# Key projection of a 32-head attention kernel: eight heads in one product instead of four heads in column strips

## The chip, the cores and the metric

The kernel runs on one core of a Trainium2 chip. The metric is the device time of one execution in microseconds (us); times of several executions are given as their median. A profile is the record of one execution. Engines are named as the profile names them: PE (TensorE, matrix products), PEld (its weight loads), DVE (VectorE), ACT (ScalarE), POOL (GpSimd) and SP (SyncE, which here only issues DMAs).

## What is computed

One input x of 2048 rows and 512 columns (bf16) goes through two attention blocks with 32 heads of 16 columns each, and a gate per row mixes the two results.

```python
q, k, v = (x @ wqkv) split into 32 heads of 16            # for A and for B, each with its own wqkv
A: scores = q k^T / 4; p = softmax(scores); o = p v       # full, 2048 x 2048 for each head
B: the same over 8 keys per row: row s sees s, s-2, ..., s-14
a = o_A @ A_wo;  b = o_B @ B_wo
g = sigmoid(sum(x * gate_w))
out = g * a + (1 - g) * b
```

Block A holds nearly all the work: 32 heads of 2048 by 2048 scores, each of which needs one exponential.

## The kernel before, in words

**Units and sets.** The 32 heads are eight groups of four (group i holds heads 4i to 4i+3), and the 2048 query rows are four chunks of 512 (QW). A period is one group with one chunk; there are 32 periods, all eight groups of chunk 0 first. A period has 64 units: one unit is 128 keys of one head against the 512 queries. For each unit PE computes scores into one PSUM bank, an engine takes the exponential, and PE multiplies the result with the values and sums into the accumulator bank of the period. ACT does 1709 of the 2048 units in 684 activations (L1314, here "exps", counted from 0 as ex0, ex1, ...), alternately of three and of two units; the two PSUM rings `rA` (three banks) and `rB` (two) hold their scores, so that one is filled while the other is read. DVE does the other 339 units by integer arithmetic (L1242, L1261). Period 1 begins at ex24, period 2 at ex48, period 3 at ex72, period 4 at ex95, period 5 at ex118, period 6 at ex140, period 7 at ex162.

**The other three PSUM banks** ("misc") are shared by everything else: the accumulator of the running period (two at a change of period), all projections, the scores of DVE's units, transposes. A bank is given back when DVE has copied it out.

**Keys.** A score product takes 32 of PE's 128 rows (a row strip, one for each of four heads). In those 32 rows of `kt_all` a head has its 16 key rows and 16 *bound rows*: rows that hold minus the largest absolute key entry, one for each column. They meet |q| in the query tile, so that the product comes out as the score less an upper bound of it, and the exponential can't overflow. `k_proj` (L644) projects the keys of one group and one chunk: four contraction steps, and in each, four products of 32 output columns, one in each column strip of the array (`mm_k`, L378). 16 of the 32 columns of a strip are the head's own keys, the other 16 are those of a neighbour head and serve the bound. `kc` (L656) copies the bank into `kt_all` and takes the row maxima along. `k_bound` (L663) reduces the maxima, moves them to the right rows by two tiny products with `perm`, and `fill` (L679) writes them over the 16 bound rows. Heads 3 of the groups need a weight tile of their own, `wk3`, which DVE and POOL copy at the start (`k3`, L587).

**Queries.** From period 2 on, `q_pair` (L788) projects the queries of two groups at once: eight heads of 16 columns fill all 128 output columns, with the plain slice of `wq` as weights. DVE copies out q (`qs`) and |q| (`qa`), SP writes both to a scratch tensor in DRAM (`put`, L811, one DMA each), and two more DMAs (`get`, L818) read each group's 128 rows back, q and |q| interleaved per head.

**What sets the order.** Every piece of work is an `op` with an engine, a guessed duration, a due time (`dl`), an earliest time (`rel`), what it depends on and which buffers it takes. `list_schedule` (L175) runs through guessed time and, per engine, takes from the operations that can start the one that is due first; the instructions are then emitted in that order, and each engine executes its own in order. Keys of group i are due 14 us (by the guess) ahead of their first period and may not start before 12 us ahead of the start of the previous group (L699). Where PE would stand idle by the guess, the planner puts in products with zeros (L1472) that keep PE active.

Of the kernel before, what the change touches and what calls it, by code (L numbers as in the profile page):

```python
# [9 lines left out]
ALU = mybir.AluOpType  # L10
AX = mybir.AxisListType
FP32 = mybir.dt.float32
BF16 = mybir.dt.bfloat16
# [14 lines left out]
DH = 16  # L28
NG = 8
W = 8  # L30
DIL = 2
QW = 512
# [4 lines left out]
DEXP = -2.0565  # L37
NV = 4
NGR = 3
ROW = QW + 2  # L40
NPT = 3
NGA = 3
# [9 lines left out]
def _ap(base, dims):  # L52
    return bass.AP(tensor=base.tensor, offset=base.offset, ap=[list(d) for d in dims])
# [53 lines left out]
SB = lambda n: [(True, 0.065 + n / 3840.0)]  # L107
# [4 lines left out]
WAVE = lambda n: PASS * n  # L112
# [189 lines left out]
def kernel(  # L302
# [15 lines left out]
    S, D = x2d.shape  # L318
    assert D == 512 and S % QW == 0
    NT = S // 128  # L320
    NC = S // QW
    DC = D // 128
# [6 lines left out]
    const = ctx.enter_context(tc.tile_pool(name="const", bufs=1))  # L329
# [5 lines left out]
    def misc_ps(shape, dtype=FP32, tag="misc"):  # L335
        if tag in ("misc", "acc"):
            bank, = [tk.bank for tk in now[0].alloc if isinstance(tk.res, Banks)]
            tag = f"m{bank}"
        return ps.tile(shape, dtype, tag=tag, bufs=1, name="misc_ps")
# [27 lines left out]
    V = Chained(nc.vector, "dve")  # L367
    A = Chained(nc.scalar, "act")
    G = Chained(nc.gpsimd, "pool")
    SP = Chained(nc.sync, "sp")  # L370

    def mm(out, lhsT, rhs, start, stop, **kw):
        return chain(nc.tensor.matmul(out, lhsT=lhsT, rhs=rhs, start=start, stop=stop, **kw))  # L373
# [16 lines left out]
    def op(eng, occ, fn, dl, **kw):  # L390
        if any(tk.kind == "misc" for tk in kw.get("use", ())):
            dl -= URG[eng]
        o = Op(eng, occ, fn, dl, **kw)
        ops.append(o)
        return o
# [3 lines left out]
    def tok(tag, cap):  # L399
        name = "banks" if tag in ("misc", "acc") else tag  # L400
        if name not in res:
            res[name] = Banks(3) if name == "banks" else Res(cap)
        return Tok(res[name], tag)
# [53 lines left out]
    S0 = [T0 + UNIT * f for f in first_unit]  # L457

    wkv = const.tile([128, DC, 2 * D], BF16, name="wkv")
    wq = const.tile([128, DC, D], BF16, name="wq")  # L460
    wq2 = const.tile([128, DC, 8, 2, DH], BF16, name="wq2")
    q_scr = tc.dram_tile([NG * NC // 2 * 16, DH * QW], BF16, name="q_scr")
    wk3 = const.tile([128, DC, NG, 2, DH], BF16, name="wk3")
    a_w3 = A_wqkv.rearrange("(c p) n -> p c n", p=128)
    gw = const.tile([128, DC], BF16, name="gw")
    bw = const.tile([128, DC, 3 * D], BF16, name="bw")
    bwo = const.tile([128, DC, D], BF16, name="bwo")
# [7 lines left out]
    rowc = const.tile([128, 3], FP32, name="rowc")  # L475
    wts = const.tile([128, NV - 1], BF16, name="wts")
    z32 = const.tile([128, 32], BF16, name="z32")
    z_bc = _ap(z32[:, 0:1], [list(z32[:].ap[0]), [0, QW]])
    perm = const.tile([128, 2, 4, 2, DH], BF16, name="perm")
    qmask = const.tile([128, 1], U32, name="qmask")  # L480
    xT = const.tile([128, DC, S], BF16, name="xT")
    kt_all = const.tile([128, NG, S], BF16, name="kt_all")
    vp_all = const.tile([128, NT, H, DH + 1], BF16, name="vp_all")
    vd_all = const.tile([128, NV - 1, NTD, H, DH + 1], BF16, name="vd_all")
    kmax_all = const.tile([128, NG, NC], FP32, name="kmax_all")
    kmax_b = const.tile([128, NG], BF16, name="kmax_b")
    negk = const.tile([128, NG], FP32, name="negk")
# [29 lines left out]
    def init_perm():  # L517
        idv = ident[:].rearrange("p (a b d) -> p a b d", a=4, b=2)
        G.memset(perm[:], 0.0)
        G.tensor_copy(out=perm[:, 0, :, 1, :], in_=idv[:, :, 0, :])  # L520
        G.tensor_copy(out=perm[:, 1, 1:4, 1, :], in_=idv[:, 0:3, 1, :])
        G.tensor_copy(out=perm[:, 1, 0, 1, :], in_=idv[:, 3, 1, :])

    def init_pool2():
        make_identity(nc, identf)
# [11 lines left out]
    o_perm = op("pool", 1.0, init_perm, -8.5, deps=[o_id])  # L537
    o_init_p = op("pool", 2.8, init_pool2, -8.0, deps=[o_perm])
# [37 lines left out]
    o_wk = op("sp", 0.5, load_w(1), -8.9, lat=6.5)  # L576
# [10 lines left out]
    def k3(E, i0, i1):  # L587
        def s():
            wk = wkv[:, :, 0:D].rearrange("p c (i j d) -> p c i j d", i=NG, j=4)
            for e, j in ((0, 3), (1, 0)):  # L590
                E.tensor_copy(out=wk3[:, :, i0:i1, e, :], in_=wk[:, :, i0:i1, j, :])
        return s
# [6 lines left out]
        return s  # L599

    o_k3 = [op("dve", 0.2, k3(V, 0, 1), -4.0, deps=[o_wk])]
    o_k3 += [op("pool", 2.0, k3(G, 1, NG), -3.0, deps=[o_wk, o_init_p])] * (NG - 1)
    o_q2 = [op("dve", 0.5, q2(V, 0), 0.0, deps=[o_wq]), op("pool", 1.5, q2(G, 1), 5.0, deps=[o_wq, o_k3[1]])]

    def warm():
# [5 lines left out]
    o_xt = []  # L611
    for sc in range(NC):
        st = {}
# [76 lines left out]
            o_k[i] = [op("dve", 0.0, fill(0, S), dl, deps=[c], parts=SB(S))] * NC  # L690

    o_k = {}
    for i in range(NG):
        o_kc[i] = []
        for sc in range(NC):
            if i == 0:
                o_kc[i].append(k_proj(i, sc, ("misc", "acc", "misc", "misc")[sc], -2.0 + sc))
            else:
                o_kc[i].append(k_proj(i, sc, "misc", S0[i] - 14.0 - 3.5 * (NC - 1 - sc), rel=S0[i - 1] - 12.0 if i > 1 else K1REL))  # L699
        k_bound(i, 2.0 if i == 0 else S0[i] - 11.0)  # L700
# [87 lines left out]
    def q_pair(pi, dl, rel):  # L788

        c_, i = periods[pi]  # L790
        st = {}
        tk, tqs, tqa = tok("misc", 2), tok("qs", 1), tok("qa", 1)

        def part(c0, c1):
            def s():
                if c0 == 0:
                    st["p"] = misc_ps([128, QW])
                for c in range(c0, c1):
                    mm(st["p"][:], wq[:, c, 4 * i * DH:4 * (i + 2) * DH], xT[:, c, c_ * QW:(c_ + 1) * QW], c == 0, c == DC - 1)
            return s  # L800

        def ev():
            st["s"] = work.tile([128, QW], BF16, name="qs", tag="qs", bufs=1)
            V.tensor_copy(out=st["s"][:], in_=st["p"][:])

        def ab():
            st["a"] = work.tile([128, QW], BF16, name="qa", tag="qa", bufs=1)
            V.tensor_scalar(out=st["a"][:].bitcast(U32), in0=st["s"][:].bitcast(U32), scalar1=0x7FFF7FFF, scalar2=None,
                            op0=ALU.bitwise_and)

        def put(e):  # L811
            def s():
                src = st["sa"[e]]
                SP.dma_start(out=_ap(q_scr[8 * pi + e:8 * pi + e + 1, :], [[2 * DH * QW, 8], [QW, DH], [1, QW]]),
                             in_=src[:])
            return s

        def get(e):  # L818
            def s():
                qt_tiles[pi + e] = work.tile([128, QW], BF16, name="qt", tag="qt", bufs=4)  # L820
                SP.dma_start(out=qt_tiles[pi + e][:], in_=_ap(q_scr[8 * (pi + e):8 * (pi + e) + 1, :], [[QW, 128], [1, QW]]))
            return s
        a = op("pe", WAVE(2), part(0, 2), dl - 8.6, full=2, deps=[o_wq] + o_xt[c_], alloc=[tk], rel=rel, name=f"qp{pi}")
        a = op("pe", WAVE(2), part(2, DC), dl - 8.0, full=2, deps=[a], use=[tk], name=f"qp{pi}")
        c = op("dve", 0.61, ev, dl - 7.0, deps=[a], alloc=[tqs], use=[tk])
        b = op("dve", 0.0, ab, dl - 6.8, deps=[c], alloc=[tqa], use=[tqs], parts=SB(QW))
        w = [op("sp", 0.5, put(0), dl - 5.0, deps=[c], use=[tqs], lat=2.2), op("sp", 0.5, put(1), dl - 4.0, deps=[b], use=[tqa], lat=2.2)]
        for e in range(2):
            q_tok[pi + e] = tok("qt", 4)
            o_q[pi + e] = op("sp", 0.5, get(e), dl - 1.0 + e, deps=w, alloc=[q_tok[pi + e]], lat=2.2)  # L830
# [34 lines left out]
    a = None  # L865
    for sc in range(NC):
        a = op("pe", 0.9, zmm(sc), GT + sc, full=1, deps=[o_bw, a] + o_xt[sc], alloc=[tzp] if sc == 0 else [],
               use=[tzp] if sc else [], rel=20.0)
    a = op("act", 0.25, zsig, GT + 5, deps=[a], use=[tzp])
    o_g = op("dve", 0.8, zgate, GT + 6, deps=[a])  # L870
    a = op("pe", 1.2, zrows, GT + 8, full=1, deps=[o_g, o_init_p], alloc=[tzr])
# [427 lines left out]
    for k, us in enumerate(sets):  # L1299
# [6 lines left out]
        st = dict(k=k, us=us, tn=tn, tp=tp)  # L1306
# [7 lines left out]
        def ex(st=st, n=n, k=k):  # L1314
# [4 lines left out]
        a = op("pe", 0.0, qk, tn - 3.0, mode="r", js=[u_[2] for u_ in us], deps=[o_q[pi] for pi in pis] + kd,  # L1319
               alloc=[tr_], use=[q_tok[pi] for pi in pis], after=[last_qk[0]], scores=k % 2, name=f"qk{k}")  # L1320
# [15 lines left out]
    for pi, (c_, i) in enumerate(periods):  # L1336
        st = {}
# [32 lines left out]
        a = op("dve", 0.64, po1, E - PO1D, deps=o_pv[pi], alloc=[ta], use=[acc_tok[pi], acc_two[pi]])  # L1370
        tr_ = tok("rden", 2)
        a = op("dve", 0.29, po2, E + 4.0, deps=[a], alloc=[tr_], use=[ta])
        al, us = [to] if i % 2 == 0 else [], [ta, tr_] + ([to] if i % 2 else [])
        if by_v:
            a = op("dve", 0.0, po2a, E + 4.0, deps=[a, o_gr], use=[tr_], parts=TT(BPC))
            a = op("dve", 0.0, po2b, E + 4.0, deps=[a], alloc=al, use=us, parts=TT(BPC * DH))
        else:
            a = op("pool", 0.0, po2a, GFIRST, deps=[a, o_gr], use=[tr_], parts=GP("ff", BPC))
            a = op("pool", 0.0, po2b, GFIRST, deps=[a], alloc=al, use=us, parts=GP("ff", BPC * DH))
# [12 lines left out]
    for t in range(NT):  # L1392
        c_, tt = t // TPC, t % TPC
        st = {}
# [122 lines left out]
```

## Time and profile before

| what | value |
|---|---|
| median of 3 runs | 815.02 us (814.9 to 815.13) |
| profiled execution, its own time | 816.37 us |
| profiled execution, span from first to last instruction | 814.6 us |
| mean granted PE clock | 0.997 of full |
| ACT busy | 786.8 us (97%), of it 778.7 us in 684 exps |
| PE busy | 754.1 us (93%), 6969 products recorded |
| DVE busy | 685.0 us (84%) |
| POOL busy | 633.1 us (78%) |
| ex0 starts, last exp ends | 18.5 us, 806.6 us |

The profiled execution took 1.8 us more than its span, and 1.35 us more than the median of the runs. An engine's share of busy time is a mean over the whole span; in the first 215 us, in which all keys and values are projected, PE has more to do than later.

### The profile page before, as it was taken

The numbers are of one execution on the slowest core, as the hardware profiler recorded it, in microseconds if no ns is written. First come the engines' busy times: TensorE is split into PE (matmuls) and PEld (weight loads), VectorE is DVE, ScalarE is ACT, GpSimd is POOL, SyncE is SP. The second block draws the span as 40 slices with busy tenths as digits, with TensorE's granted clock in tenths as the row PEclk, the third lists the DMA queues.
The fourth block names the chain that finished last, engine by engine and source line by source line (L and its number), as shares of the span: only waits on it lengthen the run. The fifth ranks groups of instructions, "written<-read, shape, count | busy, mean of one in ns | idle before, by whom it ended". The sixth has DMA issues, their size and how long they took to land.

```text
span 814.6 us, 18016 instructions
## 1 busy us (share of the span) xinstructions
PE 754.1 (93%) x6969; PEld 247.2 (30%) x7022; DVE 685.0 (84%) x1068; ACT 786.8 (97%) x708; POOL 633.1 (78%) x1058
## 2 busy tenths in 40 slices
PE   8989999999999999989899999899989998999997
PEld 5343333323222222222232222223222222322322
DVE  5636787787988999989988899998989699999796
ACT  3999999999999999999999999999999999999996
POOL 3097979997998999999997894979789219998910
PEclk9999999999999999999999999999999999999999
DMA  8503081544344354444524516162442321522000
GB/s 261 140 5 118 2 180 42 149 111 104 93 100 127 104 118 130 110 112 107 132 54 111 136 33 163 34 162 54 91 130 50 81 86 58 144 59 72 1 2 27
DMA packets 58886, 77.22 MB, mean 95 GB/s; under 512 B 3744, under 2 KB 50848, under 8 KB 58800
## 3 DMA queue, kind: packets, MB, share of 16 engines
q1 hardware_dynamic: 52608, 53.91, 21.4%
q0 software_dynamic: 6048, 22.02, 14.8%
q8 instruction: 55, 0.90, 0.5%
q14 instruction: 31, 0.25, 0.1%
q10 hardware_dynamic: 144, 0.13, 0.0%
HBM read 43.78 MB, written 10.26 MB: 66 GB/s over the span
## 4 chain that ended last, share of the span: by engine, by line
ACT 49%; PE 24%; issue 21%; DVE 3%; DMA 2%; SPq 1%; ACTq 0%; DVEq 0%
ACT pT L364 48%; PE misc_ps L373 16%; PE ring L373 8%; DMA xld<-in_A_x_dram 1%; ACT lg L364 1%; SPq L364 1%; DMA woarr<-in_A_wo_dram 0%; DVE pd_a L364 0%; DMA q_scr<-qa 0%; DVE accT L364 0%; PE pxt L621 0%; DVE qs L364 0%; DVE qa L364 0%; DVE kt_all L364 0%; DVE kvs L364 0%
## 5 line engine op out<-in xcount | busy, mean ns | idle before, releaser
L364 ACT ACTIVATE pT<-ring 128x1536 bf16<-128x1536 f32 (+1 forms) x684 | 778.7, 1329 | 12.1 <-PE ring L373 9.3
L373 PE MATMUL ring<-qt,kt_all 32*128 32x512 bf16 x1709 | 268.7, 382 | 46.7 <-ACT pT L364 39.0
L364 POOL TENSOR_TENSOR prod<-ksh,qb 128x256 f32<-128x256 bf16 x256 | 174.0, 729 | 58.0 <-DMA ksh<-kv_scr 53.2
L373 PE MATMUL misc_ps<-pT,vp_all 128*17 128x512 bf16 (+1 forms) x1709 | 205.6, 384 | 1.7 <-DVE accT L364 1.1
L373 PEld LDWEIGHTS <-kt_all 32*128 32x128 bf16 x2048 | 88.2, 91 | 294.9 <-issue 286.4
L364 DVE TENSOR_SCALAR pd_a<-wkv 128x1536 uint16<-128x1536 uint16 x192 | 175.0, 941 | 0.9 <-PE misc_ps L373 0.4
L364 POOL TENSOR_TENSOR prod<-prod 128x256 f32<-128x256 f32 (+1 forms) x256 | 167.2, 668 | 5.6
L364 DVE TENSOR_SCALAR wkv<-misc_ps 128x512 uint16<-128x512 f32 x192 | 128.7, 683 | 26.8 <-PE misc_ps L373 24.1
L373 PE MATMUL misc_ps<-z 128*32 128x512 bf16 x425 | 138.2, 387 | 1.6 <-DVE z L364 1.6
L364 DVE TENSOR_SCALAR pd_a<-dt_a 128x1536 uint16<-128x1536 uint16 x147 | 135.2, 943 | 1.8 <-PE misc_ps L373 1.1
L373 PE MATMUL misc_ps<-pd_a,vd_all 128*17 128x512 bf16 x1017 | 130.9, 381 | 0.4 <-DVE pd_a L364 0.2
L373 PE MATMUL misc_ps<-qt,kt_all 32*128 32x512 bf16 x339 | 124.2, 381 | 1.3 <-DVE kt_all L364 0.4
L364 DVE TENSOR_SCALAR dt_a<-misc_ps 128x512 uint16<-128x512 f32 x147 | 98.8, 683 | 26.6 <-PE misc_ps L373 25.0
L364 POOL TENSOR_TENSOR prod<-vsh,lg 128x256 f32<-128x256 bf16 x128 | 84.2, 758 | 0.0
L373 PEld LDWEIGHTS <-vp_all 128*17 128x17 bf16 (+1 forms) x2048 | 55.1, 88 | 87.0 <-issue 73.2
L364 POOL TENSOR_TENSOR av<-vsh,lg 128x256 f32<-128x256 bf16 x128 | 78.2, 646 | 0.0
L373 PE MATMUL misc_ps<-bw,xT 128*128 128x512 bf16 x164 | 51.7, 389 | 1.1 <-issue 0.5
L373 PEld LDWEIGHTS <-z 128*32 128x32 bf16 x425 | 37.5, 96 | 48.2 <-issue 24.8
L373 PEld LDWEIGHTS <-vd_all 128*17 128x17 bf16 x1017 | 34.5, 88 | 48.2 <-issue 39.4
L373 PEld LDWEIGHTS <-xT 128*128 128x128 bf16 x576 | 29.1, 97 | 34.0 <-issue 31.0
L373 PE MATMUL misc_ps<-xT,wkv 128*32 128x512 bf16 x384 | 36.6, 381 | 0.0
L373 PE MATMUL misc_ps<-xT,wk 128*32 128x512 bf16 x128 | 35.8, 381 | 0.0
(89 smaller groups left out, 554.0 us busy)
## 6 DMA issues: line engine op xcount, KB each, us to landing
ksh<-kv_scr SPq DMA_DIRECT2D x32, 512.0 KB
vsh<-kv_scr SPq DMA_DIRECT2D x32, 512.0 KB
av<-prod POOLq DMA_DIRECT2D x28, 512.0 KB, 5.7
av<-av POOLq DMA_DIRECT2D x14, 512.0 KB, 5.3
kv_scr<-kvs SPq DMA_DIRECT2D x16, 256.0 KB
qt<-q_scr SPq DMA_DIRECT2D x30, 128.0 KB
q_scr<-qs SPq DMA_DIRECT2D x15, 128.0 KB
q_scr<-qa SPq DMA_DIRECT2D x15, 128.0 KB
```

Of the source, the lines that this page charges most:

```text
L364: return chain_on(key, f(*a, **k))
L373: return chain(nc.tensor.matmul(out, lhsT=lhsT, rhs=rhs, start=start, stop=stop, **kw))
```

## The change

Keys of groups 0 and 1 stay as they were. Those of groups 2 to 7 are made by pairs (2 and 3, 4 and 5, 6 and 7) by a new function `k_pair`: one product of 128 columns per contraction step holds the keys of eight heads, ordered so that each strip of 32 rows has 16 rows of the even group's head and 16 rows of the odd group's head. Two DVE copies follow: the first copies the bank into `kt_all` for the even group, the second copies the same rows, negated, for the odd group, and reads them from the even group's rows in SBUF (`KSB`), not from PSUM. Each takes row maxima along. Since the second is negated, the maxima of both give the largest absolute value of both groups, and one chain of reduction, two tiny products and one small DVE operation serves both groups; two `fill` operations then write the bound rows, over the odd group's keys in the even group and over the even group's keys in the odd one. So odd groups have their bound rows first and their keys second, and the queries of odd groups must be laid out likewise: each `put` of a pair from group 2 on becomes two DMAs of 64 rows, the second with q and |q| exchanged. The weights come from a new tile `wkp`, which POOL fills at the start by eight copies (`kpw`), and `wk3` shrinks to groups 0 and 1. A pair's keys are due at the date of its even group, so the odd group's come a period earlier than before.

```diff
-    wk3 = const.tile([128, DC, NG, 2, DH], BF16, name="wk3")
+    wk3 = const.tile([128, DC, NK1, 2, DH], BF16, name="wk3")
+    wkp = const.tile([128, DC, (NG - NK1) // 2, 4, 2, DH], BF16, name="wkp")
...
+        G.tensor_copy(out=perm[:, 2, :, 0, :], in_=idv[:, :, 1, :])
...
-    o_k3 += [op("pool", 2.0, k3(G, 1, NG), -3.0, deps=[o_wk, o_init_p])] * (NG - 1)
+    o_k3 += [op("pool", 0.6, k3(G, 1, NK1), -3.0, deps=[o_wk, o_init_p])] * (NK1 - 1)
+    def kpw():
+        wk = wkv[:, :, 4 * NK1 * DH:D].rearrange("p c (i e j d) -> p c i e j d", e=2, j=4, d=DH)
+        for c in range(DC):
+            for e in range(2):
+                G.tensor_copy(out=wkp[:, c, :, :, e, :], in_=wk[:, c, :, e, :, :])
+    o_kp = op("pool", 2.0, kpw, 6.0, rel=12.0, deps=[o_wk, o_k3[1]])
...
+    def k_pair(i, dl, rel):
+        cs = []
+        for sc in range(NC):
...
+                    for c in range(c0, c1):
+                        mm(st["p"][:], wkp[:, c, (i - NK1) // 2].rearrange("p j e d -> p (j e d)"), xT[:, c, sc * QW:(sc + 1) * QW],
+                           c == 0, c == DC - 1)
...
+            def ev(e, st=st, sc=sc):
+                def s():
+                    src = kt_all[:, i, sc * QW:(sc + 1) * QW] if e and KSB else st["p"][:]
+                    V.tensor_scalar(out=kt_all[:, i + e, sc * QW:(sc + 1) * QW], in0=src, scalar1=(1.0, -1.0)[e], scalar2=None,
+                                    op0=ALU.mult, op1=ALU.max, accum_out=kmax_all[:, i + e, sc:sc + 1])
+                return s
+            d = dl - KPS * (NC - 1 - sc)
+            a = op("pe", WAVE(2), part(0, 2), d - 1.8, full=2, deps=[o_kp] + o_xt[sc], alloc=[tk], rel=rel, name=f"kp{i}.{sc}")
+            a = op("pe", WAVE(2), part(2, DC), d - 1.2, full=2, deps=[a], use=[tk], name=f"kp{i}.{sc}")
+            a = op("dve", 0.61, ev(0), d, deps=[a], use=[tk])
+            cs += [a, op("dve", 0.61, ev(1), d + 0.3, deps=[a], use=[] if KSB else [tk])]
...
+        def mx():
+            V.tensor_reduce(out=kmax_b[:, i:i + 1], in_=kmax_all[:, i:i + 2, :], axis=AX.XY, op=ALU.max)
+        def sw():
+            st["p"] = misc_ps([128, 2])
+            for e in range(2):
+                mm(st["p"][:, e:e + 1], perm[:, 2 * e].rearrange("p a b d -> p (a b d)"), kmax_b[:, i:i + 1], True, True)
+        def ng():
+            V.tensor_scalar(out=negk[:, i:i + 2], in0=st["p"][:], scalar1=-1.0, scalar2=None, op0=ALU.mult)
...
+                V.tensor_scalar(out=kt_all[:, i + e, :], in0=kt_all[:, i + e, :], scalar1=rowc[:, 1 + e:2 + e],
+                                scalar2=negk[:, i + e:i + e + 1], op0=ALU.mult, op1=ALU.add)
...
-    for i in range(NG):
+    for i in range(NK1, NG, 2):
+        k_pair(i, S0[i] - (KPD if i > 2 else KP2), S0[i - 1] - KPR if i > 2 else KP1)
+    for i in range(NK1):
...
+                if i < NK1:
...
+                for g_ in range(2):
+                    r0 = 8 * (pi + g_) + (e ^ g_)
+                    SP.dma_start(out=_ap(q_scr[r0:r0 + 1, :], [[2 * DH * QW, 4], [QW, DH], [1, QW]]),
+                                 in_=src[64 * g_:64 * g_ + 64, :])
```

The constants are KPD, KPS, KPR, KP1, KP2 = 16.0, 3.5, 20.0, 44.0, 11.0.

More of the change, by code (lines that the diff above doesn't have):

```diff
@@ L39 @@
 NGR = 3
+NK1 = 2
+KSB = True
+KPD, KPS, KPR, KP1, KP2 = 16.0, 3.5, 20.0, 44.0, 11.0
 ROW = QW + 2
@@ L478 @@
     z_bc = _ap(z32[:, 0:1], [list(z32[:].ap[0]), [0, QW]])
-    perm = const.tile([128, 2, 4, 2, DH], BF16, name="perm")
+    perm = const.tile([128, 3, 4, 2, DH], BF16, name="perm")
     qmask = const.tile([128, 1], U32, name="qmask")
@@ L692, with part, s, fill @@
     o_k = {}
-    for i in range(NG):
+    def k_pair(i, dl, rel):
+        cs = []
+        for sc in range(NC):
+            st = {}
+            tk = tok("misc", 2)
+            def part(c0, c1, st=st, sc=sc):
+                def s():
+                    if c0 == 0:
+                        st["p"] = misc_ps([128, QW])
+                    for c in range(c0, c1):
[3 more added lines that the diff above has]
+            def ev(e, st=st, sc=sc):
+                def s():
+                    src = kt_all[:, i, sc * QW:(sc + 1) * QW] if e and KSB else st["p"][:]
+                    V.tensor_scalar(out=kt_all[:, i + e, sc * QW:(sc + 1) * QW], in0=src, scalar1=(1.0, -1.0)[e], scalar2=None,
+                                    op0=ALU.mult, op1=ALU.max, accum_out=kmax_all[:, i + e, sc:sc + 1])
+                return s
+            d = dl - KPS * (NC - 1 - sc)
[3 more added lines that the diff above has]
+            cs += [a, op("dve", 0.61, ev(1), d + 0.3, deps=[a], use=[] if KSB else [tk])]
+        st = {}
+        tk = tok("misc", 2)
+        def mx():
[6 more added lines that the diff above has]
+            V.tensor_scalar(out=negk[:, i:i + 2], in0=st["p"][:], scalar1=-1.0, scalar2=None, op0=ALU.mult)
+        def fill(e):
+            def s():
+                V.tensor_scalar(out=kt_all[:, i + e, :], in0=kt_all[:, i + e, :], scalar1=rowc[:, 1 + e:2 + e],
+                                scalar2=negk[:, i + e:i + e + 1], op0=ALU.mult, op1=ALU.add)
+            return s
+        m = op("dve", 0.2, mx, dl + 0.5, deps=cs)
+        m = op("pe", 0.1, sw, dl + 1.0, full=0, deps=[m, o_perm], alloc=[tk])
+        m = op("dve", 0.2, ng, dl + 1.8, deps=[m], use=[tk])
+        for e in range(2):
+            o_k[i + e] = [op("dve", 0.0, fill(e), dl + 3.0 + 20.0 * e, deps=[m], parts=SB(S))] * NC
@@ L813, in s @@
                 src = st["sa"[e]]
-                SP.dma_start(out=_ap(q_scr[8 * pi + e:8 * pi + e + 1, :], [[2 * DH * QW, 8], [QW, DH], [1, QW]]),
-                             in_=src[:])
+                if i < NK1:
+                    SP.dma_start(out=_ap(q_scr[8 * pi + e:8 * pi + e + 1, :], [[2 * DH * QW, 8], [QW, DH], [1, QW]]),
+                                 in_=src[:])
+                    return
+                for g_ in range(2):
+                    r0 = 8 * (pi + g_) + (e ^ g_)
+                    SP.dma_start(out=_ap(q_scr[r0:r0 + 1, :], [[2 * DH * QW, 4], [QW, DH], [1, QW]]),
+                                 in_=src[64 * g_:64 * g_ + 64, :])
             return s
@@ L826, in q_pair @@
         b = op("dve", 0.0, ab, dl - 6.8, deps=[c], alloc=[tqa], use=[tqs], parts=SB(QW))
-        w = [op("sp", 0.5, put(0), dl - 5.0, deps=[c], use=[tqs], lat=2.2), op("sp", 0.5, put(1), dl - 4.0, deps=[b], use=[tqa], lat=2.2)]
+        np_ = 0.5 if i < NK1 else 1.0
+        w = [op("sp", np_, put(0), dl - 5.0, deps=[c], use=[tqs], lat=np_ + 1.7),
+             op("sp", np_, put(1), dl - 4.0, deps=[b], use=[tqa], lat=np_ + 1.7)]
         for e in range(2):
```

## The prediction

> **What bounds the kernel now.** I read the page first: the shares of the engines, then the costliest group of ACT.
>
> ```profile
> PE 754.1 (93%) x6969; PEld 247.2 (30%) x7022; DVE 685.0 (84%) x1068; ACT 786.8 (97%) x708; POOL 633.1 (78%) x1058
> ...
> L364 ACT ACTIVATE pT<-ring 128x1536 bf16<-128x1536 f32 (+1 forms) x684 | 778.7, 1329 | 12.1 <-PE ring L373 9.3
> ```
>
> The reader is to see that ACT's 684 exps take 778.7 us and that ACT stood idle 12.1 us in all ahead of them. The change gives ACT neither more nor fewer units, so those 778.7 us stay. What it can win is idle time of ACT between ex0 and the last exp: 12.1 less the 4.4 us ahead of ex0, so 7.7 us, 0.9% of the whole. Where they lie is told by ACT's timeline from 50 to 175 us (columns: start, length of the merged row, what, how many, and in brackets the idle time ahead of its first):
>
> ```profile
> 54.54 13.75 ACT L364 ACTIVATE pT<-ring 128x1536 bf16<-128x1536 f32 x12 [1.45 <-PE misc_ps L373]
> 68.55 8.23 ACT L364 ACTIVATE pT<-ring 128x1536 bf16<-128x1536 f32 x7 [0.26 <-PE ring L373]
> ...
> 83.37 22.71 ACT L364 ACTIVATE pT<-ring 128x1536 bf16<-128x1536 f32 x20 [0.86 <-PE ring L373]
> 107.27 2.37 ACT L364 ACTIVATE pT<-ring 128x1536 bf16<-128x1536 f32 x2 [1.19 <-PE ring L373]
> ...
> 112.56 23.03 ACT L364 ACTIVATE pT<-ring 128x1536 bf16<-128x1536 f32 x20 [0.29 <-PE misc_ps L373]
> 136.59 20.45 ACT L364 ACTIVATE pT<-ring 128x1536 bf16<-128x1536 f32 x18 [1.00 <-PE ring L373]
> ...
> 167.97 8.35 ACT L364 ACTIVATE pT<-ring 128x1536 bf16<-128x1536 f32 x7 [1.38 <-PE ring L373]
> ```
>
> Seven stalls hold 6.4 of the 7.7 us, and all seven lie before 170 us, while keys and values are projected; between 213 and 775 us ACT's timeline has no stall over 0.1 us. So after 213 us PE may get faster or slower by a little and nothing follows. Next, PE's timeline ahead of the stall that ends at 107.27 us:
>
> ```profile
> 105.07 0.40 PE L373 MATMUL misc_ps<-xT,wkv 128*32 128x512 bf16 x3
> 105.16 0.38 PE L373 MATMUL misc_ps<-xT,wk 128*32 128x512 bf16 x1
> 105.28 0.40 PE L373 MATMUL misc_ps<-xT,wkv 128*32 128x512 bf16 x3
> 105.38 0.38 PE L373 MATMUL misc_ps<-xT,wk 128*32 128x512 bf16 x1
> 105.50 0.47 PE L373 MATMUL misc_ps<-pT,vp_all 128*17 128x512 bf16 x4
> 105.72 0.40 PE L373 MATMUL misc_ps<-xT,wkv 128*32 128x512 bf16 x3
> ...
> 106.77 0.60 PE L373 MATMUL ring<-qt,kt_all 32*128 32x512 bf16 x5
> ```
>
> Rows `xT,wkv` and `xT,wk` with 128*32 are the key strips of `mm_k`. One contraction step (three strips and one) begins every 0.215 us: 105.07, 105.28, and so on. From 105.07 to 106.77 PE does six such steps, three half-products, with one product of values between, and ACT's next scores (`ring`) come only then. Two exps in a row take 2.28 us (a row of ACT's timeline without stalls has 36 of them in 41.09 us), and PE must bring five units of scores in that time. In PE's instruction order the stall of 83.37 (ex54) has two key half-products ahead of its scores, that of 107.27 (ex74) three, that of 112.56 (ex78) two, that of 136.59 (ex98) four, that of 68.55 (ex42) one beside two projections of block B. The other two (ex30 and ex124, 1.45 and 1.38 us) have none.
>
> **The change part by part.**
>
> *PE, removed.* Groups 2 to 7 took 6 x 4 chunks x 4 steps = 96 steps; three pairs take 48 full products. A full product costs a step too: two of them (`xT,wq`) begin at 103.27 and the scores after them at 103.86, 0.59 us, which is 2 x 0.215 and one change of array form. So 48 x 0.215 = 10.3 us of PE go, nearly all between ex29 and ex150. Three of six bound chains go with them.
>
> *PE, added.* Strips stand beside the products of values, also in column strips, with no pause (105.28 to 105.50 is one step). A full product doesn't: from the scores at 102.95 to `xT,wq` at 103.27 are 0.32 us, 0.105 over a step. The Trainium skill, TensorEngine Tiling (Array Packing), section Key Properties, speaks against this change here: a change of tiling mode, not merely of tile, drains the array. At two changes for each of the 24 half-products the row's price makes 24 x 2 x 0.105 = 5.0 us, at most half of what was saved; and counted in the built order there are 35 more changes of form than before up to ex160, 3.7 us. The page gives no price of its own. Zero products go from 425 to 429, 0.9 us.
>
> *The order.* What counts is not the sum but the heaps. In the order of the changed program the key half-products stand at ex35 to ex44, ex66 to ex76 and ex106 to ex115, never more than two between the scores of one three-unit set and the next. So the terms are: ex54 0.86, ex74 1.19, ex78 0.29, ex98 1.00 and ex42 0.26 us go, **3.6 us**. The stall at ex30 stays, since the two orders are the same up to there; just behind it one more half of a value projection comes ahead of ex32 in place of two key halves (the piece `wkv,xT` with 32 products at 51.53 takes 1.11 us, two halves 0.86): **0.25 us** back. The stall at ex124 has no key product; its row is bounded by 0 and 1.38 us gained. PE there waited 1.10 us for DVE, which still had |q| (1.17 us), the accumulator and one of its own units ahead of it, and a bank was held by the bound of group 6; then PE's clock was down (below). In the new order that query pair stands twelve sets earlier and the bound two, which speaks for a gain; but another heap may come at another period's change. I take half, **0.7 us**.
>
> *DVE.* As many copies as before. 12 of 24 read SBUF: no row shows that with row maxima. Bounds: 0.35 us (the bound fill of 512 columns, 128x512, takes 407 ns, four in 1.38 us) and 0.83 us (copy from PSUM with maxima 745 ns and its readout 82 ns). I take the latter, the same instruction. DVE had 16 to 21 us of work in 25 in this stretch, so nothing follows; a bank is free after the first copy, and only 12 banks are taken for keys in place of 24. The fill of an odd group comes a period early.
>
> *POOL at the start.* Eight copies of 128x192: between 0.17 us (`perm`, 128x64) and 0.37 us (`wq`, 128x256), say 0.3 each, 2.4 us, less 0.7 for the smaller `wk3`. POOL was idle 4.71 us from 7.5 us on, waiting for `wq`; that hides it. Without that cover it would delay only POOL's first products, which wait for `ksh`. One `perm` copy lies ahead of an idle 0.61 us. Block B ends at 776 us on POOL, and its last tile is wanted at 803 us.
>
> *SP.* 12 pairs x 2 = 24 DMAs more, at 0.58 us of issue each (`q_scr<-qa`), so a `get` and what stands behind it, loads of block B and outputs, come 1.2 us later. The gets were issued at least 16 us ahead of their period (116.2 for period 4 at 132.3, 506.0 for period 20 at 522.1), and the wait for the landing of a `put` was 3.4 us on average (51.1 us in 15) and 8.2 at most: hidden. If that cover were gone, all of 1.2 us times 12 would show.
>
> *Sum.* 3.6 - 0.25 + 0.7 = 4.05 us. Against the profiled execution: 816.37 - 4.05 = 812.3; against the median, which lies 1.35 us below it: 815.02 - 4.05 = **811.0 us**. The start (18.5 us) and the tail (8 us after the last exp) keep their order.
>
> **The rivals.**
>
> *The stalls belong to the change of period.* All of ex30, ex54, ex74, ex98 and ex124 lie two to six sets after the start of a period (24, 48, 72, 95, 118), when two accumulators leave one bank for all else, and ex30 shows it without any key strip. Then other work fills the place, and only ex42 and ex78 go: 815.02 - 0.55 = 814.5 us. Against it: ahead of 107.27 PE has no idle row, it is busy with strips. Chance 0.19.
>
> *PE's clock falls (slower).* With fewer steps and more waits PE may look idle. The windows view shows it once in mid-run (last figures: granted clock, DMA share, GB/s):
>
> ```profile
> 160.00:165.00 5.00, 3.83 (x31) 1.21 (x28) 4.63 (x8) 4.89 (x5) 4.48 (x8) 0.92 0.62 105
> 165.00:170.00 5.00, 5.00 (x41) 1.54 (x39) 4.22 (x6) 3.62 (x4) 4.95 (x8) 0.73 0.20 55
> ```
>
> At half clock that is 2 x (5 x 0.08 + 5 x 0.27) = 3.5 us, and ACT lost 1.38 us in it. [...] Each window more costs 1.4 us; four more turn 811.0 into 816.6, just where slower begins, and five make it 818.0. Against: the stretches after 213 us have about as little beside the scores and keep 1.00. Chance 0.13.
>
> *More is gained.* All stalls after ex30 go: 7.7 - 1.45 - 0.2 (before ex30) = 6.0, so 809.0 us, or a little less. Chance 0.06 for less than that.
>
> **How the numbers follow.** Forecast 0.62, rivals 0.19, 0.13 and 0.06. A measurement of this kernel tells 0.2%, 1.6 us, from no change. Faster is the forecast and the last rival, 0.68; within 0.2% the first rival, 0.19; slower 0.13. The range leaves out the slower case, a little of the first rival and what is below 808.9: 808.9 to 815.6.
>
> **What would show it.** Right: ACT's timeline has no stall over 0.5 us between 56 and 160 us; `xT,wkp` x48 with about 390 ns; ACT's idle time ahead of exps near 8 us in place of 12.1. Wrong: stalls at the same sets after the same work, a clock row under 1.00 in several windows, or `qt` landing after its period has begun.

## The result, and the profile after

The changed kernel takes 812.26 us (median of 6 runs, 810.97 to 813.55) against 815.0 us (814.9 to 815.13): a ratio of 0.9965, with a 95% interval of 0.9953 to 0.9977. Run once more beside the kernel before it took 811.68 us against 814.97: 0.995 [0.9938, 0.9962]. It is faster by 2.7 to 3.3 us; 4.0 were forecast.

The page of the profile after (811.8 us of span, 813.55 us for the execution, the longest of the six), and the costliest group of ACT:

```profile
PE 744.2 (92%) x6625; PEld 240.1 (30%) x6684; DVE 684.3 (84%) x1062; ACT 786.3 (97%) x708; POOL 634.7 (78%) x1067
...
L367 ACT ACTIVATE pT<-ring 128x1536 bf16<-128x1536 f32 (+1 forms) x684 | 778.3, 1347 | 9.4 <-PE ring L376 5.5
```

PE has 9.9 us less work by the records, where 10.3 less 0.9 for zeros were forecast (just under 1% of the products are missing from both records, so the last digit isn't firm). ACT's exps take the same 778 us; its idle time ahead of them fell from 12.1 to 9.4 us, 2.7 us, nearly the whole difference of the spans (814.6 and 811.8). ACT's timeline after, all rows of exps from ex24 on with 0.19 us or more of idle time ahead, up to 300 us:

```profile
54.84 20.45 ACT L367 ACTIVATE pT<-ring 128x1536 bf16<-128x1536 f32 x18 [1.45 <-PE misc_ps L376]
...
123.58 2.49 ACT L367 ACTIVATE pT<-ring 128x1536 bf16<-128x1536 f32 x2 [0.19 <-PE ring L376]
126.77 29.57 ACT L367 ACTIVATE pT<-ring 128x1536 bf16<-128x1536 f32 x26 [0.70 <-PE ring L376]
264.71 14.92 ACT L367 ACTIVATE pT<-ring 128x1024 bf16<-128x1024 f32 x13 [1.33 <-PE misc_ps L376]
```

The five stalls that were put down to heaps of key strips are gone (ex42, ex54, ex74, ex78, ex98). The one of ex30 stands as it did, 1.45 us. The 1.38 us of ex124 are gone too, and 1.33 us stand at 264.71 (ex211) instead, 100 us later, where no key is made. Those of 123.58 and 126.77 (ex90 and ex92) are new. The rows of the changed operations:

```profile
L376 PE MATMUL misc_ps<-xT,wkp 128*128 128x512 bf16 x45 | 13.3, 383 | 0.4 <-issue 0.3
...
L367 DVE TENSOR_SCALAR_CACHE_REDUCE kt_all<-misc_ps 128x512 bf16<-128x512 f32 x12 | 8.2, 685 | 3.8 <-PE misc_ps L376 3.7
L367 DVE TENSOR_SCALAR_CACHE_REDUCE kt_all<-kt_all 128x512 bf16<-128x512 bf16 x12 | 8.0, 676 | 0.2
```

Three of the 48 full products are missing from this record; the second profile of the changed kernel has all 48, 383 ns each.

### The profile page after: what moved, and what is told of

Same layout as the page of the kernel before. It is cut to its first block, busy times and chain, and to the rows that moved or that the text cites. A ratio compares the mean times of both kernels' runs of the same rounds, so it can differ in the third digit from the quotient of the medians.

```text
span 811.8 us, 17373 instructions
## 1 busy us (share of the span) xinstructions
PE 744.2 (92%) x6625; PEld 240.1 (30%) x6684; DVE 684.3 (84%) x1062; ACT 786.3 (97%) x708; POOL 634.7 (78%) x1067
## 4 chain that ended last, share of the span: by engine, by line
ACT 52%; issue 21%; PE 19%; DVE 6%; POOL 1%; DMA 1%; SPq 0%; ACTq 0%
ACT pT L367 51%; PE misc_ps L376 13%; PE ring L376 6%; DVE pd_a L367 2%; DVE wkv L367 1%; DVE dt_a L367 1%; DMA xld<-in_A_x_dram 1%; ACT lg L367 1%; POOL prod L367 1%; DVE vd_all L367 1%; DVE kt_all L367 0%; POOL av L367 0%; PE pxt L633 0%; DVE oat L367 0%; DVE qa L367 0%
## 5 line engine op out<-in xcount | busy, mean ns | idle before, releaser
L367 POOL TENSOR_TENSOR prod<-ksh,qb 128x256 f32<-128x256 bf16 x256 | 171.6, 726 | 63.8 <-DMA ksh<-kv_scr 31.9
L376 PEld LDWEIGHTS <-kt_all 32*128 32x128 bf16 x2048 | 90.4, 91 | 309.0 <-issue 300.5
L367 POOL TENSOR_TENSOR prod<-prod 128x256 f32<-128x256 f32 (+1 forms) x256 | 172.1, 691 | 5.6
L376 PEld LDWEIGHTS <-vp_all 128*17 128x17 bf16 (+1 forms) x2048 | 53.1, 88 | 83.6 <-issue 72.4
L376 PE MATMUL misc_ps<-bw,xT 128*128 128x512 bf16 x159 | 49.5, 383 | 2.6 <-issue 1.7
L367 DVE CAST kvs<-misc_ps 128x512 bf16<-128x512 f32 x32 | 21.8, 682 | 11.7 <-PE misc_ps L376 11.7
L367 DVE STREAM_TRANSPOSE accT<-misc_ps 128x512 f32<-128x512 f32 x32 | 22.7, 708 | 10.0 <-PE misc_ps L376 10.0
```

Source lines behind the costliest of these rows:

```text
L367: return chain_on(key, f(*a, **k))
```

## The experiments

**The spread of the executions.** The median of the kernel before hides two sorts of execution. Three sets of runs give 56 executions of it with the granted clock of each. 40 have a mean clock of 0.999 or 1.000 and take 814.68 to 815.31 us (median 814.98). 14 have 0.997 or 0.998 and take 815.92 to 816.51. Two have 0.996 and take 817.4 and 817.68. The profiled execution of before (816.37 us, 0.997) was of the second sort: it has a half-clock window (a stretch in which PE is granted half its clock) at 164 us, and the stall of 1.38 us with it. That window lasts 3.41 us and takes 0.002 off the mean clock, so the 40 executions at 0.999 or 1.000 had no such window. A clock of 0.998 doesn't tell by itself: the profile of the run with the bank held (below) has 0.998 and no window before the end of the execution.

**Two pairs in place of three, and one** (`NK1` alone is changed, to 4 and to 6).

```diff
-NK1 = 2
+NK1 = 4
```

> Groups 4 to 7 are made as pairs (NK1 = 4), groups 2 and 3 stay in strips. Theory heaps: the stalls at ex42 (0.26) and ex54 (0.86) stay, those at ex74, ex78 and ex98 (2.48 us in all) go: about 812.5 to 813.3 as long as there is one half-clock window somewhere. Rival, the pairing of groups 2 and 3 gives the most because it comes where PE is fullest: 814 or more.

Measured: 813.91 us (812.65 to 815.98, 11 runs), ratio 0.9985 [0.9974, 0.9996]. Its five executions with a clock of 0.999 or 1.000 take 812.65 to 812.90. The median lies between the two expectations, so the stalls have to decide. ACT's timeline (profiled execution, clock 1.000):

```profile
68.45 8.23 ACT L367 ACTIVATE pT<-ring 128x1536 bf16<-128x1536 f32 x7 [0.26 <-PE ring L376]
83.27 24.97 ACT L367 ACTIVATE pT<-ring 128x1536 bf16<-128x1536 f32 x22 [0.86 <-PE ring L376]
108.60 1.45 ACT L367 ACTIVATE pT<-ring 128x1536 bf16<-128x1536 f32 x1 [0.36 <-PE ring L376]
113.71 41.02 ACT L367 ACTIVATE pT<-ring 128x1536 bf16<-128x1536 f32 x36 [0.19 <-PE ring L376]
```

As expected, ex42 and ex54, where groups 2 and 3 are still strips, keep their 0.26 and 0.86 us to the hundredth; behind them 0.55 us are left of 2.48.

> Only groups 6 and 7 are made as a pair (NK1 = 6); groups 2 to 5 stay in strips. Theory heaps (ACT's stalls of 0.86, 1.19, 0.29, 1.00 and 0.26 us at ex54, ex74, ex78, ex98 and ex42 come from key strips piled ahead of scores): the built order has the same heaps as before up to ex98, so the stalls at ex42, ex54, ex74, ex78 and ex98 stay and the time stays at 815.0 within 0.7 us, or less by 1.4 us if the half-clock window near 164 us goes. Rival, bank and period change (fewer copies hold banks, whatever the order): a third of the gain of the whole change, 0.9 us.

Measured: 820.82 us (820.62 to 825.89, 6 runs), ratio 1.0082 [1.0064, 1.01]. Up to ex98 the stalls are those of before, as expected. But the time is 5.8 us over before, which neither theory gave. In its profile ACT's exps lost 11.4 us between ex0 and the last, against 7.7. Two new stalls are where key halves stand close, three, three and two ahead of ex116, ex118 and ex120. But the halves are not all that stands there: PE also waited 0.69 us (up to 158.72) and 0.97 us (up to 161.94) for copies of keys on DVE, nearly as long as the stalls. The copies came behind an |q| that began at 153.47 and took 4.59 us beside a run of seven POOL products; the shortest |q| in this profile takes 0.28 us (more on this in the last section).

```profile
160.20 2.37 ACT L367 ACTIVATE pT<-ring 128x1536 bf16<-128x1536 f32 x2 [0.75 <-PE ring L376]
163.61 11.84 ACT L367 ACTIVATE pT<-ring 128x1536 bf16<-128x1536 f32 x10 [1.04 <-PE ring L376]
```

Another 3.0 us went between 455 and 475 us, far from any key, most of it in a stretch at half clock (windows view, granted clock third from the right):

```profile
465.00:470.00 5.00, 4.31 (x22) 0.99 (x22) 4.89 (x9) 4.39 (x4) 4.61 (x10) 0.68 0.24 83
470.00:475.00 5.00, 5.00 (x41) 1.10 (x39) 3.48 (x5) 3.09 (x3) 4.92 (x9) 0.64 0.00 0
```

So a small edit lets the planner lay out the rest anew. One execution with a clock of 0.998 also took 820.62, so not all of the 5.8 us hang on the clock; the rest was not followed up.

**The same order with PE's old time for keys.**

```diff
-                        mm(st["p"][:], wkp[:, c, (i - NK1) // 2].rearrange("p j e d -> p (j e d)"), xT[:, c, sc * QW:(sc + 1) * QW],
-                           c == 0, c == DC - 1)
+                        w_ = wkp[:, c, (i - NK1) // 2].rearrange("p j e d -> p (j e d)")
+                        x_ = xT[:, c, sc * QW:(sc + 1) * QW]
+                        for r_ in (x_, z_bc) if c == 0 else (z_bc, x_):
+                            mm(st["p"][:], w_, r_, c == 0 and r_ is x_, c == DC - 1 and r_ is x_)
```

> The changed kernel with its order unchanged, but each of the 48 full key products is followed or preceded by one with zeros as the moving side that adds nothing: PE's time for keys is that of before (48 x 0.215 = 10.3 us more), while the dates, the banks, the copies and the planner's order are those of the changed kernel. Theory heaps, PE's time: each half-product is 0.43 us longer and stalls come back where two stand together (ex38 to ex46, ex68 to ex78, ex108 to ex116), 1.5 to 3.5 us, so 813.5 to 816. Rival, the order and the dates: the time stays at 811 to 813.

Measured: 819.75 us (818.56 to 821.29, 5 runs), ratio 1.0059 [1.0047, 1.0071], 7.5 us over the changed kernel. The stalls come back where key halves stand; PE's and ACT's timelines around one of them:

```profile
70.54 0.39 PE L376 MATMUL misc_ps<-z,wkp 128*128 128x512 bf16 x1
70.77 0.38 PE L376 MATMUL misc_ps<-xT,wkp 128*128 128x512 bf16 x1
...
72.06 0.38 PE L376 MATMUL misc_ps<-xT,wkp 128*128 128x512 bf16 x1
72.38 0.39 PE L376 MATMUL ring<-qt,kt_all 32*128 32x512 bf16 x3
```

```profile
72.87 2.36 ACT L367 ACTIVATE pT<-ring 128x1536 bf16<-128x1536 f32 x2 [0.87 <-PE ring L376]
75.45 2.37 ACT L367 ACTIVATE pT<-ring 128x1536 bf16<-128x1536 f32 x2 [0.22 <-PE ring L376]
101.53 7.11 ACT L367 ACTIVATE pT<-ring 128x1536 bf16<-128x1536 f32 x6 [0.77 <-PE ring L376]
```

Eight steps stand between 70.54 and the scores at 72.38, and ACT waits 0.87 us for them. Together: 2.25 us from ex38 to ex46, 2.34 from ex68 to ex78, 2.17 from ex110 to ex116, where the changed kernel has none over 0.06. So 10.3 us of PE cost 6.8 us of ACT, more than the 1.5 to 3.5 expected; that fits an order that was laid out for the short products and has no room for long ones. Order and dates alone don't make the gain; PE's time does. Two limits: the run keeps the changes of array form as well, so PE has more to do in it than before the change; and pairs at the old dates were not tried, so what the shorter products alone gain stays open.

**The dates alone, with strips.**

```diff
+    KD = lambda i: S0[i] - 14.0 if i < 2 else S0[i - i % 2] - (16.0 if i > 3 else 11.0)
+    KR = lambda i: K1REL if i < 2 else S0[i - i % 2 - 1] - 20.0 if i > 3 else 44.0
...
-                o_kc[i].append(k_proj(i, sc, "misc", S0[i] - 14.0 - 3.5 * (NC - 1 - sc), rel=S0[i - 1] - 12.0 if i > 1 else K1REL))
-        k_bound(i, 2.0 if i == 0 else S0[i] - 11.0)
+                o_kc[i].append(k_proj(i, sc, "misc", KD(i) - 3.5 * (NC - 1 - sc), rel=KR(i)))
+        k_bound(i, 2.0 if i == 0 else S0[i] - 11.0 if i == 1 else KD(i) + 3.0)
```

> The kernel before, all keys in strips, but groups 2 to 7 get the due dates and earliest times that the change gives to pairs (both groups of a pair at the even group's date). Theory heaps: the same number of strips in less time makes bigger heaps (four halves ahead of ex48 and ex80), so slower than before by 1 to 3 us, 816 to 818. Rival, dates (the gain comes from when the keys are made): faster than before, 812 to 814.

Measured: 816.75 us (815.49 to 818.1, 11 runs), ratio 1.0016 [1.0008, 1.0025]. ex54, ex74 and ex98 lose their stalls here too, since the strips stand elsewhere; but where four halves were put ahead of ex48, with a value projection and two bounds, one stall of 2.84 us takes their place:

```profile
78.57 34.01 ACT L364 ACTIVATE pT<-ring 128x1536 bf16<-128x1536 f32 x30 [2.84 <-PE ring L373]
```

This profile also has a half-clock window at 583 us with 2.55 us of stalls. Leaving such executions out, the six with a clock of 0.999 or 1.000 have a median of 816.1 us, against 815.12 for the kernel before in the same set. The dates without the shorter products lose.

**The bank held for both copies** (`KSB = False`).

> The changed kernel, but the second copy of a pair reads the PSUM bank (KSB = False), so that the bank is held for both copies, 0.7 us longer. Theory heaps: the key halves stand as spread as in the changed kernel, so the time is that of the changed kernel, 811 to 813.6. Rival, banks (the gain comes from banks that are free sooner): stalls with a PE or DVE wait come back at ex40 to ex46, ex68 to ex78 and ex108 to ex116, 1 to 3 us.

Measured: 812.15 us (810.32 to 813.39, 5 runs), ratio 0.9961 [0.9949, 0.9972]: the changed kernel's time. Reading the second copy from SBUF, which takes 676 ns in place of some 685, is worth nothing that shows here.

**The query DMAs alone**, in the kernel before.

```diff
...
+                for g_ in range(2):
+                    r0 = 8 * (pi + g_) + e
+                    SP.dma_start(out=_ap(q_scr[r0:r0 + 1, :], [[2 * DH * QW, 4], [QW, DH], [1, QW]]),
+                                 in_=src[64 * g_:64 * g_ + 64, :])
```

> The kernel before, but each put of a pair from group 2 on is two DMAs of 64 rows (no exchange of halves; the layout read back is that of before). It measures the 24 DMAs alone. Theory: the gets are issued 16 us ahead of need, so nothing follows, 815.0 within 0.3 us. Rival: 24 x 0.58 us of issue delay loads of block B and cost up to 2 us.

Measured: 815.78 us (815.23 to 818.06, 11 runs), ratio 1.001 [1.0001, 1.0019], about 0.5 us, more than the 0.3 that the expectation left. ACT's stalls in its profile are those of before, one by one within 0.12 us. Where the 0.5 us lie stays open.

**Zeros against the half-clock window.** First in the kernel before, five products with zeros ahead of the wait near 162 us:

```diff
-            for _ in range(st["op"].filled):
+            for _ in range(st["op"].filled + (0 if first else {116: 2, 117: 3}.get(gs[0]["k"], 0))):
```

> The kernel before in its own order, with five more zero products into the running accumulator just ahead of the value products that precede PE's wait near 162 us (two at pv116, three at pv117). Theory clock: the half-clock window at 164 to 168 us follows from little PE work just before it; with 5 x 0.215 us more work there it goes away in some or all executions, and with it the 1.38 us stall at ex124: 813.6 to 814. Rival: that stall comes from the work ahead of ex124 and not from the clock: 815.0 or a little more.

Measured: 815.56 us (815.35 to 816.76, 11 runs), ratio 1.0002 [0.9994, 1.0011]. The profiled execution has no window and no stall at ex124, and 2 of 11 executions have a clock of 0.997 (816.7 us), where 8 of 27 of before beside it are under 0.999: too few to show that the zeros make the window rarer. The other nine take 815.35 to 815.77, 0.4 us more than before's of that sort. The time is the rival's, 815.0 or a little more: the expected 813.6 to 814 took 1.38 us from a median that does not contain them.

Then in the changed kernel:

> The changed kernel in its own order, with six more zero products into the running accumulator near 258 to 262 us (one at pv202 and pv203, one ahead of each of four DVE units' scores). Theory clock: the half-clock window at 261 to 265 us goes, and the 1.33 us stall there: a median of 810.8 to 811.3, and executions that agree better than 810.97 to 813.55. Rival: it only moves to another place, 812.3.

Measured: 812.61 us (811.4 to 813.51, 5 runs), ratio 0.9965 [0.9951, 0.9978]. It is over the 810.8 to 811.3 expected, but the trial missed its place: only four zeros came into the program, none of them between 257 and 261 us, and the window stayed (260.4 us, stall 1.29 us). The next two put them ahead of the products for DVE's units themselves, eight as in this diff, and fourteen (4, 4, 4 and 2):

```diff
...
+            for _ in range({(8, 8): 2, (8, 9): 2, (8, 10): 2, (8, 11): 2}.get((pi, dq_n[pi]), 0)):
+                mm(acc_tiles[zp][32 * free[0]:32 * free[0] + 32, :], z32[:], z_bc, False, False, tile_position=(0, 32 * free[0]))
             mm(st["x"][:], kt_all[32 * j:32 * j + 32, i, t * 128:(t + 1) * 128], qt_tiles[pi][32 * j:32 * j + 32, :],
```

> The changed kernel in its own order with eight zero products into the open accumulator, two ahead of each of the four products for DVE's units between 259 and 261 us, where PE stood waiting for banks and did 25 products in 3.42 us (the first trial put only four, and none of them there). Theory clock: PE is busier by 8 x 0.215 = 1.7 us in the 3.4 us ahead of the half-clock window, the window at 261 us goes in most executions, and the median is 811.0 to 811.7. Rival: the stall at ex211 is made by the work there: 812.3 or, with the zeros, more.

Measured: 811.95 us (811.4 to 813.89, 6 runs), ratio 0.9961 [0.9949, 0.9972], between the two expectations. In the profiled execution the window at 261 us and its 1.33 us are gone; 0.79 us at ex209 and ex210 stand in their place, and in this execution another window at 360 us.

> As the run with eight zero products, with fourteen (four, four, four and two), 3.0 us of PE in the same place. Theory clock: the window goes, but the zeros now come ahead of scores and cost 0.5 to 1.3 us of stall at ex208 to ex212 themselves: 811.5 to 812.5. If eight were too few to move the clock and fourteen do it, the difference shows the point.

Measured: 813.09 us (812.69 to 814.48, 6 runs), ratio 0.9975 [0.9964, 0.9986]. No window ahead of the tail in the profile, but ACT waits for the zeros:

```profile
260.72 1.02 ACT L367 ACTIVATE pT<-ring 128x1024 bf16<-128x1024 f32 x1 [0.96 <-PE ring L376]
262.88 7.05 ACT L367 ACTIVATE pT<-ring 128x1536 bf16<-128x1536 f32 x6 [1.14 <-PE ring L376]
```

2.1 us in place of 1.33, more than the 0.5 to 1.3 expected, and so is the time. The stall at ex211 goes with the window: the profiles of this order that have a window there have the stall (1.33 us; 1.29 in the first trial; 0.89 with doubled products and the window at 268.66 us), and those of the last two trials and of the changed kernel once more (below) have neither. That the zeros take the window away isn't shown, since the last of these profiles is without it and has no added zeros. What fills PE there stands ahead of scores, and neither of the last two trials beats the changed kernel beside them (811.68 us).

**The changed kernel once more.**

> The changed kernel once more, unaltered, for its executions and their mean granted clock. Theory clock: executions with a mean clock of 0.999 or 1.000 take 811.0 to 811.6 and those with 0.997 take 812.2 to 813.0, 1.3 us more, where the kernel before takes 815.0 with the former and 816.3 with the latter; the median depends on which sort is the more frequent. Rival, the spread is something else: no such tie. And the 4.28 us operation on DVE at 117 us with the stalls of 0.70 and 0.19 us behind it was a matter of that execution: not seen here.

Measured: 811.68 us (810.11 to 812.06, 5 runs). Of the eleven executions of the changed kernel in both sets, five have a clock of 0.999 or 1.000: 810.11 to 811.69, median 811.08. Six have 0.997 or 0.998: 811.66 to 813.55, median 812.27. The tie holds, less sharply than before the change. As expected, the operation of 4.28 us (1.85 here) and the stalls of 0.70 and 0.19 us at ex92 and ex90 are not in this profile; 0.97 us at ex154 are (0.14 in the first).

## Why the prediction was right, and where it was not

*The heaps of key strips, 3.6 us.* Right. The five stalls went; with two pairs only those of the pairs went; with PE's old time for keys they came back at the new places. Like against like, executions at a clock of 0.999 or more: 814.98 before, 812.65 to 812.90 with two pairs, 811.08 with three. That is 3.9 us, 0.3 more than this term alone; in the one set of runs that has both kernels side by side it is 3.5 us (814.89 and 811.38), so the 0.3 is no more than sets differ by.

*"The stalls belong to the change of period."* Only ex30 does; the rival fell.

*0.25 us back at ex32.* Not there: neither profile of the changed kernel has a stall of 0.06 us at ex31 to ex33, so this term is nil.

*The stall at ex124, half of 1.38 us, 0.7 us.* This term failed, as the prediction put it against the median: "816.37 - 4.05" and "815.02 - 4.05" took the same sum from both. But the 1.35 us by which the profiled execution stood over the median match this very stall. Most executions of before have a mean clock that leaves no room for the window, and so nothing to gain from the stall. None of these was profiled; the nearest is the run with five zeros, whose profile has neither window nor stall. It should have been read from the two numbers side by side: an excess of 1.35 us over runs that agree within 0.23 us, a stall of 1.38 us and a clock row under 1.00 in the profile.

*"PE's clock falls".* It came in part, far below its price of four windows: six of eleven executions of the changed kernel have a clock under 0.999, against 16 of 56 before. Eleven are few (five of the first six, one of the last five), so it isn't shown that the change made windows more frequent. With 1.2 us between the medians of the two sorts, that share took a part of the gain back: 811.08 for the one sort, 811.69 for all eleven. The prediction held against this rival that the stretches after 213 us keep full clock; the window after lies at 261 us.

What brings a window stays open. The Trainium skill, TensorE: Matmul & The Clock Gate, section Why this matters for your kernels, warns of idle gaps of PE over some 3 us between bursts of products. These windows came without one: PE's longest wait in the 3.42 us ahead was 1.10 us before and 0.43 us after. Nor is it little work alone. PE's busy time (the second figure) ahead of the window of before:

```profile
160.83:164.25 3.42, 2.25 (x22) 0.90 (x19) 3.38 (x8) 3.31 (x5) 3.05 (x6) 1.00 0.60 115
```

And of after, first ahead of its window, then in a later stretch that no window followed:

```profile
257.96:261.38 3.42, 2.37 (x25) 0.90 (x18) 2.48 (x5) 3.42 (x4) 3.34 (x7) 1.00 0.17 57
565.16:568.58 3.42, 2.27 (x27) 0.86 (x25) 1.67 (x3) 3.42 (x4) 3.34 (x7) 1.00 0.00 0
```

2.25 and 2.37 us of work came ahead of windows, 2.27 us did not, so busy time alone doesn't decide. The clock records of the traces show a beat, though: in one execution the windows begin whole multiples of 3.413 us apart (before at 164.25 and, as the work ends, 812.78, 190 times; after at 261.38 and 810.92, 161 times; with doubled products at 268.66 and 528.07, 76 times). If PE's work is counted in such a beat, and the beat falls differently on each execution, one lean stretch is cut differently each time. That would explain two sorts of execution of one program; it was not tested.

*Changes of array form, 3.7 us of PE.* Hidden in the room that the shorter products left: no stall over 0.06 us at any of the key halves. *DVE.* The unknown copy from SBUF took 676 ns and 82 ns of readout, 0.76 us, inside 0.35 to 0.83 and near the end that was taken. But "so nothing follows" held in neither profile of the changed kernel: slow DVE operations (last section) stood ahead of 0.89 us of stalls at ex90 and ex92 in the first, and of 0.97 us at ex154 in the second. *POOL.* 2.37 us for the eight copies, 2.4 forecast, hidden. *SP.* Hidden in the trace, the gets 13.3 us or more ahead of need; by the run with the DMAs alone perhaps 0.5 us.

## What to carry to other kernels

In a kernel whose bound engine is fed in a fixed beat, shorter work elsewhere pays only where it stood in a heap ahead of the feed: list the bound engine's stalls, look what its feeder did just before each, and count only those. Before a stall is put into a sum, ask whether it is in the runs that the sum is held against; a profiled execution that stands over tight runs by the length of one stall probably has that stall where they don't; the mean clock of each run helps to tell. And where an order is planned, any edit lays out the rest anew, with stalls in places that the edit doesn't touch.

## What the runs showed of the hardware

One DVE operation between SBUF tiles can take over twice its time in one execution beside a busy POOL and not in the next, in the same order of instructions. The weighted copy of values (`vd_all`, 128x1632) took 1.85 to 2.33 us nearly everywhere, but 3.0 us in the run with doubled products and 4.28 us in the first profile of the changed kernel, where the stalls of ex90 and ex92 followed:

```profile
116.82 4.28 DVE L367 TENSOR_TENSOR vd_all<-vp_all,wts 128x1632 bf16<-128x1632 bf16 x1
```

POOL was at work nearly all that time. Two of its products ended at 119.29 us; its next, of 128x128, ran from 119.00 to 121.35, 2.35 us in place of 0.39 in the second profile, and ended 0.25 us after DVE's operation. So first DVE was late, by some 2.4 us, and then POOL.

In the second profile |q| took 2.13 us beside a run of four POOL products, in place of 1.31 in the first, and ended 0.15 us after the last of the four (in the first, 0.16 us after the last of its four; the shortest |q| in both takes 0.28 us); the stall of 0.97 us at ex154 followed:

```profile
192.80 2.13 DVE L367 TENSOR_SCALAR qa<-qs 128x256 uint32<-128x256 uint32 x1
```

```profile
192.06 2.72 POOL L367 TENSOR_TENSOR prod<-vsh,lg 128x256 f32<-128x256 bf16 x4
```

The Trainium skill, SBUF — State Buffer, section Terms, says that DVE and GpSimd arbitrate for one shared pair of SBUF ports, and that one of them holds it for a whole instruction while the loser is fully blocked. The rows of |q| and POOL agree with the blocking, but |q| waited through several POOL instructions in a row and not through one. How long an operation waits differs from execution to execution, in one and the same order (4.28 and 1.85 us for the copy of values); that POOL held the copies up was not tried by itself.
